# GpSimd's descriptor reserve cut to 1 KB, two more weight tiles, and the keys of two steps loaded instead of turned

## The chip, the core and the metric

The kernel runs on one core of a Trainium2 chip. The metric is the device time of one launch in microseconds (us); three runs of the kernel before gave 157.57 us as their median (156.55 to 157.78).

The core has a matrix engine (TensorE, PE in the profile, its weight loads PEld), a vector engine (VectorE, DVE), a scalar engine (ScalarE, ACT), GpSimd (POOL), and SyncE (SP), whose instruction queue starts every data transfer (DMA) of this kernel. 16 DMA engines carry the transfers; data passes through an on-chip memory (SBUF) that the kernel divides into pools of tiles, and matrix results through PSUM banks.

## The reference

A retention layer (linear attention with a decay for each head) over 4 batches, 8 heads, 768 positions and head width 64 makes `x`, and a soft mixture of 8 experts with 4 slots each is applied to its 3072 tokens of width 512.

```python
for t in range(S):
    state = gamma[None, :, None, None] * state + np.einsum('bhd,bhe->bhde', k[:, :, t], v[:, :, t])
    y[:, :, t] = scale * np.einsum('bhd,bhde->bhe', q[:, :, t], state)
...
logits = x @ phi                      # 3072 x 32
d = softmax of logits over the tokens
slot_input = d.T @ x                  # 32 x 512
for e in range(E):
    h = np.maximum(slot_input[e] @ w1[e], 0.0)      # w1: 8 x 512 x 1024
    slot_out[e] = h @ w2[e]                         # w2: 8 x 1024 x 512
c = softmax of logits over the slots
return (c @ slot_out)
```

Everything is float32. The two expert weights are 16.8 MB each, q, k and v 6.3 MB each, and so is the output.

## The kernel before

**The first part, the retention.** It runs in 24 steps (`NSTEP`), one for each batch and block of 128 positions, batches innermost, taken in pairs: pass `P` of the loop at L480 computes steps 2P and 2P+1 and prepares 2P+2 and 2P+3. A step needs q and k with the head's width on the partitions (`qT`, `kT`, side by side in the tile), v, and, for the state that is carried to the next block, k in its natural order (`kn`). All four have a place in one tile of 8 KB a partition from the pool `inp`, which has `NIN` = 6 tiles; so a step's load (`load_in`, called for steps 2P+6 and 2P+7) waits on SP until the step six before it has let go of its tile.

**Where `kn` comes from.** For a step in `TURNED`, `kn` isn't loaded: one DMA of 768 KB brings k, q and v (L210), and `turn_k` (L218) makes `kn` by four transposes on TensorE (L221) and one copy on ScalarE (L222). For the other steps one DMA of 1024 KB brings all four (L216). The last four steps (20 to 23) need no `kn`, and that place of their tiles takes the first w2 weights (L213).

**The order of a pass on each engine** is the order of the code, since the kernel is scheduled by hand on all engines: on TensorE `carry_mm` (L266), `attend_mm` (L275), `state_mm` (L303), `turn_k` (L221), `natural_mm` (L319), in every second pass the routing products (L399, L343), and `score_mm` of the next two steps (L242); on GpSimd the decays of the next steps' q (L227) and v (L232).

**The second part, the experts.** w1 is used in 16 tiles of 1024 KB by `hidden` (L637), w2 in 128-row pieces by the products at L715, in three blocks of output columns; each block's result is multiplied with the routing (L696), copied to output tiles (L703) and written by eight DMAs of 768 KB (L704).

**Where weights are loaded.** They have a pool `big` of `NBIG` = 13 tiles of 8 KB a partition. `PACE[P]` says how many tiles pass P asks for (`load_weights`, L483; w1 tiles are issued at L170, w2 tiles at L173). With that table passes 0 to 8 fill the 13 tiles, pass 9 asks for none, and pass 10 for two that go into tiles that steps have let go of, since from pass 9 on `weight_pool` is `inp`. The last w1 tile comes in halves (L187), early w2 pieces come behind the last steps into their tiles (`load_behind`, L193), two w2 tiles come as halves in the pool `ring` (L182). What is left, ten w2 tiles, is loaded at L173 in the loop over `hidden`, each into the tile of a w1 tile that was just used.

SP issues all of these in program order, so a load whose tile is still in use holds up all loads behind it.

**The reserve.** `_bacc.Bacc(...)` at L778 sets aside 16 KB of each partition for descriptors of DMAs that GpSimd starts. This kernel starts none from there.

Of the kernel before, what the change touches and what calls it, by code (L numbers as in the profile page):

```python
# [39 lines left out]
GRP = B  # L40
NGRP = NSTEP // GRP
ORDERED = "all"
NBIG = 13
NIN = 6
NRING = 9
PACE = (1, 1, 1, 2, 1, 2, 1, 2, 2, 0, 2, 0)
TURNED = (0, 1, 2, 3, 4, 6, 8, 10, 12, 14, 16)
SIW = 48
LEAN = [i for i in range(1, NSTEP) if i in TURNED or i >= NSTEP - B]
FULL = [i for i in range(1, NSTEP) if i not in LEAN]  # L50
# [32 lines left out]
def retention_soft_moe_kernel(  # L83
# [17 lines left out]
    inp = ctx.enter_context(tc.tile_pool(name="inp", bufs=NIN))  # L101
    big = ctx.enter_context(tc.tile_pool(name="big", bufs=NBIG))
    ps = ctx.enter_context(tc.tile_pool(name="ps", bufs=1, space=PSUM))
# [61 lines left out]
    def load_weights(n):  # L165
        for _ in range(n):
            which, *at = weights.pop(0)
            t = large(weight_pool[0])
            if which == "w1":
                nc.sync.dma_start(t, w1[tuple(at)])  # L170
                w1t[tuple(at)] = [t[:, j * 512:(j + 1) * 512] for j in range(4)]
            else:
                nc.sync.dma_start(t, w2[w2n[0]])  # L173
                w2n[0] += 1
                take(keys_of(*at), t)
# [42 lines left out]
    def turn_k(i, name):  # L218
        kp = bank(name)
        for g in range(NPAIR):  # L220
            nc.tensor.transpose(kp[:, g * 128:(g + 1) * 128], st[i]["kT"][:, g, :], ident)  # L221
        nc.scalar.copy(st[i]["kn"], kp.rearrange("p (h d) -> p h d", d=D))  # L222
# [83 lines left out]
    def state_add(P):  # L306
        for k in range(2):
            d = sst[(2 * P + k) % B]
            if P < B // 2:
                nc.scalar.copy(d, pr[P]["S"][:, k])  # L310
            else:
                nc.vector.tensor_tensor(d, d, pr[P]["S"][:, k], ALU.add)  # L312
# [167 lines left out]
    for P in range(NPP):  # L480
        last = P == NPP - 1
        g = P // 2
        load_weights(PACE[P])  # L483
        if P == NPP - 2:
# [45 lines left out]
        if P < NPP - B // 2:  # L530
            state_mm(P)
            state_add(P)
        if 2 * P + 2 in TURNED:
            turn_k(2 * P + 2, "A0")
# [255 lines left out]
```

## Time and profile before

| | before |
|---|---|
| median of three runs | 157.57 us |
| the profiled execution: its own time | 157.36 us |
| its span, first to last instruction | 155.7 us |
| TensorE busy | 143.1 us, 92% of the span |
| TensorE in the chain that ended last | 87% of the span |
| VectorE, GpSimd, ScalarE busy | 78.1, 58.7, 43.9 us |
| moved by DMA | 61.70 MB, 396 GB/s over the span |
| read from HBM, written to it | 55.05 MB, 6.29 MB |
| granted TensorE clock, mean | 0.985 |

A row of the timeline gives start and length of a run of like instructions; a DMA's start is that of its issue on SP. A row on DMA issues gives the median time from issue to landing; where the window holds one issue, it is that transfer's. Issue plus that time is when the transfer had landed, and landings of neighbours in the queue show how fast the queue drains.

### The profile page before, as it was taken

How to read it: one execution, taken by the hardware profiler on the slowest of the kernel's cores; microseconds unless marked ns; L12 is line 12 of the kernel's file. 1: busy time of each engine (PE TensorE's matmuls, PEld its weight loads, DVE VectorE, ACT ScalarE, POOL GpSimd, SP SyncE). 2: the span in 40 equal slices, each digit the busy share in tenths (PEclk: the TensorE clock that was granted, in tenths of full speed). 3: DMA queues.
4: the chain of work that ended last, by engine and by line, in shares of the span. 5: the costliest groups of instructions: out<-in, count | busy, mean ns of one | idle time of the engine just before them, and what ended most of it. 6: DMA issues, size and time to landing. Idle time of an engine off the chain costs nothing.

```text
span 155.7 us, 5529 instructions
## 1 busy us (share of the span) xinstructions
PE 143.1 (92%) x2424; PEld 106.9 (69%) x2424; DVE 78.1 (50%) x187; ACT 43.9 (28%) x104; POOL 58.7 (38%) x67
## 2 busy tenths in 40 slices
PE   7999999999999899999999979999999999999800
PEld 2689989997999678897989758865333465556400
DVE  0369327582948286564947584557520202563710
ACT  3214432425152403433232204341500000442510
POOL 1352987687838069912968085000200000000000
PEclk9999999999999999999999999999999999999985
DMA  5999999999999999999999999999999999999994
GB/s 165 414 428 418 427 407 429 405 431 406 421 411 420 416 417 417 415 415 422 400 416 412 416 414 356 350 278 374 404 434 419 432 411 425 415 411 422 389 422 174
DMA packets 10392, 61.70 MB, mean 396 GB/s; under 512 B 1152, under 2 KB 1152, under 8 KB 6016
## 3 DMA queue, kind: packets, MB, share of 16 engines
q1 hardware_dynamic: 10368, 61.35, 97.1%
q8 instruction: 19, 0.31, 0.8%
q14 instruction: 5, 0.04, 0.1%
HBM read 55.05 MB, written 6.29 MB: 394 GB/s over the span
## 4 chain that ended last, share of the span: by engine, by line
PE 87%; DMA 2%; DVE 2%; issue 2%; POOL 2%; DVEq 0%
PE A L242 15%; PE Y L275 14%; PE A L715 9%; PE A L319 7%; PE S L303 6%; PE Y L266 6%; PE Y L637 4%; PE A L637 4%; PE sm L343 4%; PE A L221 3%; PE S L399 3%; DMA b<-in_first_dram 2%; POOL b L227 2%; DVE b L703 2%; PE A L696 1%
## 5 line engine op out<-in xcount | busy, mean ns | idle before, releaser
L250 DVE TENSOR_TENSOR r<-A,mi 128x512 f32<-128x512 f32 (+1 forms) x50 | 30.2, 662 | 23.4 <-PE A L242 23.4
L227 POOL TENSOR_TENSOR b<-b,qtab 128x512 f32<-128x512 f32 x20 | 25.5, 1278 | 11.7 <-DMA b<-in_x_dram 4.3
L242 PE MATMUL A<-b 64*128 64x128 f32 x384 | 25.5, 280 | 0.3 <-DMA b<-in_first_dram 0.3
L242 PEld LDWEIGHTS A<-b 64*128 64x128 f32 x384 | 22.6, 187 | 3.6 <-issue 2.0
L232 POOL TENSOR_TENSOR b<-b,kt 128x512 f32<-128x512 f32 x23 | 23.8, 1052 | 2.2 <-DMA b<-in_x_dram 2.2
L275 PE MATMUL Y<-r,b 128*64 128x128 f32 x352 | 21.9, 276 | 0.7 <-POOL b L227 0.7
L275 PEld LDWEIGHTS Y<-r,b 128*64 128x64 f32 x352 | 19.0, 137 | 2.7 <-issue 1.5
L445 POOL TENSOR_TENSOR cn<-cn,cz 128x128 f32<-128x128 f32 x6 | 2.4, 401 | 34.1 <-DVE cz L444 17.7
L715 PE MATMUL A<-b,r 128*32 128x128 f32 (+1 forms) x352 | 14.4, 304 | 0.1
L715 PEld LDWEIGHTS A<-b,r 128*32 128x32 f32 x352 | 9.6, 110 | 6.2 <-issue 3.8
L326 ACT COPY r<-A 128x512 f32<-128x512 f32 x21 | 11.4, 595 | 4.3 <-PE A L319 4.3
L266 PE MATMUL Y<-b,sst 64*64 64x128 f32 x304 | 11.0, 276 | 1.0 <-issue 1.0
L319 PE MATMUL A<-mi,r 128*128 128x128 f32 x88 | 11.8, 276 | 0.0
L303 PE MATMUL S<-b 128*64 128x64 f32 x304 | 11.1, 222 | 0.8 <-issue 0.8
L303 PEld LDWEIGHTS S<-b 128*64 128x64 f32 x304 | 10.4, 138 | 1.1 <-issue 1.1
L319 PEld LDWEIGHTS A<-mi,r 128*128 128x128 f32 x88 | 9.7, 141 | 0.6 <-issue 0.4
L266 PEld LDWEIGHTS Y<-b,sst 64*64 64x64 f32 x304 | 8.4, 132 | 2.5 <-issue 1.3
L295 DVE COPY r<-Y 128x512 f32<-128x512 f32 x9 | 6.2, 692 | 6.7 <-PE Y L275 5.8
L703 ACT COPY b<-A 128x384 f32<-128x384 f32 x10 | 4.4, 483 | 17.2 <-PE A L696 16.2
L312 DVE TENSOR_TENSOR sst<-sst,S 128x256 f32<-128x256 f32 x16 | 6.0, 418 | 3.1 <-PE S L303 3.1
L696 PE MATMUL A<-cT,r 32*128 32x384 f32 x30 | 7.4, 526 | 0.0
L437 ACT ACTIVATE cn<-cn 128x128 f32<-128x128 f32 x6 | 1.9, 310 | 19.6 <-DVE cn L436 19.6
(154 smaller groups left out, 181.4 us busy)
## 6 DMA issues: line engine op xcount, KB each, us to landing
b<-in_w_dram SPq DMA_DIRECT2D x25, 1024.0 KB, 13.6
b<-in_x_dram SPq DMA_DIRECT2D x14, 768.0 KB, 10.0
b<-in_x_dram SPq DMA_DIRECT2D x9, 1024.0 KB, 11.0
out_dram<-b SPq DMA_DIRECT2D x8, 768.0 KB, 7.6
b<-in_wl_dram SPq DMA_DIRECT2D x4, 768.0 KB, 7.0
r<-in_w_dram SPq DMA_DIRECT2D x5, 512.0 KB, 9.6
b<-in_wq_dram SPq DMA_DIRECT2D x4, 256.0 KB, 11.3
b<-in_first_dram SPq DMA_DIRECT2D x1, 512.0 KB, 3.8
```

The source lines that it names most:

```text
L227: nc.gpsimd.tensor_tensor(q, q, qtab, ALU.mult)
L232: nc.gpsimd.tensor_tensor(v, v, vsc[:, i // B, a:b].unsqueeze(2).broadcast_to([128, b - a, D]), ALU.mult)
L242: nc.tensor.matmul(s["sc"][r][:, g, :], s["kT"][half(r), g, :], s["qT"][half(r), g, :], start=True, stop=True, skip_group_check=True)
L250: nc.vector.tensor_tensor(s["A"][:, r, g:g + n], s["sc"][r][:, g:g + n], mask.unsqueeze(1).broadcast_to([128, n, C]), ALU.mult)
L266: nc.tensor.matmul(p["y"][k][b][half(half_of(r, g)), gl, :], sst[(2 * P + k) % B][half(r), g, :], s["qT"][half(r), g, :], start=(gl == 0 a ...
L275: nc.tensor.matmul(pr[P]["y"][k][g // 2][half(half_of(r, g)), g % 2, :], s["v"][:, 2 * g + r, :], s["A"][:, r, g, :], start=(P < B // 2 an ...
L303: nc.tensor.matmul(S_[half(r), k, g, :], s["kn"][:, 2 * g + r, :], s["v"][:, 2 * g + r, :], start=True, stop=True, skip_group_check=True)
L319: nc.tensor.transpose(X[k][:, g * 128:(g + 1) * 128], pr[P]["yT"][:, k, g, :], ident)
L326: (nc.scalar.copy if engines[k] == "scalar" else nc.vector.tensor_copy)(xn, pr[P]["X"][k])
L637: nc.tensor.matmul(hp[hf][32 * j:32 * j + 32, :], si0[:, a:a + NSLOT], w1t[hf, g, k][j], start=(g == 0 and k == 0), stop=(g == 1 and k == ...
L696: nc.tensor.matmul(cp, s4[32 * j:32 * j + 32, m * 128:(m + 1) * 128], cT[32 * j:32 * j + 32, 3 * h:3 * h + 3, :], start=True, stop=True, s ...
L715: nc.tensor.matmul(op[32 * j:32 * j + 32, :w], hT[fc // 4][:, fc % 4, 4 * g + j, :], w2t[4 * g + j, cb, fc], start=(n == 0), stop=(n == le ...
```

## The change

Four edits, in three places. The reserve for GpSimd's descriptors is 1 KB a partition, not 16. The pool `big` has 15 tiles, not 13. `PACE` asks for two tiles in pass 9, which asked for none. Steps 14 and 16 leave `TURNED`, so `load_in` brings their `kn` by DMA and `turn_k` isn't called for them.

```diff
-NBIG = 13
+NBIG = 15
 NIN = 6
 NRING = 9
-PACE = (1, 1, 1, 2, 1, 2, 1, 2, 2, 0, 2, 0)
-TURNED = (0, 1, 2, 3, 4, 6, 8, 10, 12, 14, 16)
+PACE = (1, 1, 1, 2, 1, 2, 1, 2, 2, 2, 2, 0)
+TURNED = (0, 1, 2, 3, 4, 6, 8, 10, 12)
...
-    nc = _bacc.Bacc("TRN2", target_bir_lowering=False, num_devices=1)
+    nc = _bacc.Bacc("TRN2", target_bir_lowering=False, num_devices=1, dynamic_dma_scratch_size=1024)
```

On SP, the difference from the loads of step 13 to the end of the program (`b` is a tile of `inp` or `big`, `r` one of `ring`; `in_x` is a step's input, `in_w` weights):

```order
 L216 DMA b<-in_x_dram 128x2048
 L170 DMA b<-in_w_dram 128x2048
-L210 DMA b<-in_x_dram 128x1536
-L216 DMA b<-in_x_dram 128x2048
+L216 DMA b<-in_x_dram 128x2048 x2
 L170 DMA b<-in_w_dram 128x2048 x2
-L210 DMA b<-in_x_dram 128x1536
-L216 DMA b<-in_x_dram 128x2048
+L216 DMA b<-in_x_dram 128x2048 x2
 L170 DMA b<-in_w_dram 128x2048
 L216 DMA b<-in_x_dram 128x2048 x2
```

The loads of steps 14 and 16 grow from 1536 to 2048 columns, at the place in the queue where they stood. Further on, from the last step's load to the end:

```order
 L213 DMA b<-in_wq_dram 128x512
 L170 DMA b<-in_w_dram 128x2048 x2
+L173 DMA b<-in_w_dram 128x2048 x2
 L187 DMA r<-in_w_dram 128x1024
 L193 DMA b<-in_wl_dram 128x1536 x2
@@ -40,5 +39,5 @@
 L193 DMA b<-in_wl_dram 128x1536 x2
 L182 DMA r<-in_w_dram 128x1024 x4
-L173 DMA b<-in_w_dram 128x2048 x10
+L173 DMA b<-in_w_dram 128x2048 x8
 L704 DMA out_dram<-b 128x1536 x8
```

Two tiles of 1024 KB move from the ten behind the first expert products to the place ahead of the last w1 tile: pass 9 now loads the two w1 tiles that pass 10 loaded, and pass 10 two w2 tiles. On TensorE, pass 6 before, from the state's products to the scores of step 14:

```order
L303 MATMUL S<-b 64x64 x16
L221 MATMUL A_995<-mi,b 128x128 x4
L319 MATMUL A_1001<-mi,r 128x128 x4
L319 MATMUL A_1006<-mi,r 128x128 x4
L379 MATMUL sm<-mi,pT 128x128
L242 MATMUL A_1018<-b 128x128
```

and now:

```order
L303 MATMUL S<-b 64x64 x16
L319 MATMUL A_995<-mi,r 128x128 x4
L319 MATMUL A_1000<-mi,r 128x128 x4
L379 MATMUL sm<-mi,pT 128x128
L242 MATMUL A_1012<-b 128x128
```

The four transposes at L221 are gone here, as in pass 7, and with each four the copy at L222 on ScalarE. GpSimd's order is the same.

## Rows read from the trace of the kernel before

**Rows 1.** DMA queue of the data transfers, whole span: packets, MB, share of engines.

```profile
q1 hardware_dynamic: 10368, 61.35, 97.1%
```

**Rows 2.** Stretches: length; PE, PEld, DVE, ACT, POOL busy (count); clock, DMA share, GB/s.

```profile
94.00:99.00 5.00, 5.00 (x89) 4.42 (x89) 2.77 (x6) 1.93 (x4) 1.45 (x3) 1.00 0.96 374
99.00:104.00 5.00, 5.00 (x97) 3.71 (x89) 2.64 (x8) 1.97 (x6) 0.00 (x0) 1.00 0.91 267
...
109.00:146.00 37.00, 36.31 (x574) 18.01 (x562) 11.17 (x33) 7.70 (x17) 0.80 (x2) 1.00 1.02 419
```

**Rows 3.** Timeline of SP, 94 to 109 us: start, length, engine, line, transfer, count.

```profile
94.61 0.83 SPq L193 DMA_DIRECT2D b<-in_wl_dram  x2
99.43 0.33 SPq L187 DMA_DIRECT2D sst<-in_w_dram  x1
100.48 1.78 SPq L193 DMA_DIRECT2D b<-in_wl_dram  x2
...
108.68 0.33 SPq L173 DMA_DIRECT2D b<-in_w_dram  x1
```

**Rows 4.** DMA issues at 94.61, 99.43, 100.48, 108.68: size, us to landing.

```profile
b<-in_wl_dram SPq DMA_DIRECT2D x1, 768.0 KB, 5.8
...
sst<-in_w_dram SPq DMA_DIRECT2D x1, 512.0 KB, 4.9
...
b<-in_wl_dram SPq DMA_DIRECT2D x1, 768.0 KB, 6.9
...
b<-in_w_dram SPq DMA_DIRECT2D x1, 1024.0 KB, 8.4
```

**Rows 5.** Issues at 3.33, 3.83; 61.32, 61.77; 113.83, 114.69; q8 in 0:71, 0:133, 94:109.

```profile
b<-in_x_dram SPq DMA_DIRECT2D x1, 768.0 KB, 10.0
...
b<-in_x_dram SPq DMA_DIRECT2D x1, 1024.0 KB, 13.2
...
b<-in_x_dram SPq DMA_DIRECT2D x1, 1024.0 KB, 6.8
...
b<-in_x_dram SPq DMA_DIRECT2D x1, 1024.0 KB, 10.4
...
b<-in_w_dram SPq DMA_DIRECT2D x1, 1024.0 KB, 18.2
...
b<-in_w_dram SPq DMA_DIRECT2D x1, 1024.0 KB, 20.5
...
q8 instruction: 9, 0.15, 0.9%
...
q8 instruction: 17, 0.28, 0.9%
...
q8 instruction: 2, 0.03, 1.1%
```

**Rows 6.** The chain that ended last, passes 7, 9 and 10: start, us, what.

```profile
69.06 0.59 PE A L221 x4
69.64 0.87 PE A L319 x8
...
85.76 1.02 PE A L319 x8
...
91.65 1.04 issue
```

**Rows 7.** Sixth output's issue; its landing; the very first load's landing.

```profile
146.59 0.33 SPq L704 DMA_DIRECT2D out_dram<-b  x1
...
out_dram<-b SPq DMA_DIRECT2D x1, 768.0 KB, 4.6
...
b<-in_first_dram SPq DMA_DIRECT2D x1, 512.0 KB, 3.8
```

**Rows 8.** Step 23: GpSimd's decay of q; the chain's row of its scores.

```profile
91.79 1.27 POOL L227 TENSOR_TENSOR b<-b,qtab 128x512 f32<-128x512 f32 x1 [0.74 <-DMA b<-in_x_dram]
...
97.25 1.09 PE A L242 x16
```

## The prediction

> **What bounds the kernel now.** I read the DMA queue first. The data queue moves 61.35 MB [rows 1]. In a stretch in which it is always fed, 109 to 146 us, it moves 419 GB/s [rows 2]. 61.35 MB at that rate are 146.4 us of a span of 155.7, so the queue has 9 us to spare in the whole execution, the start and the last landing among them. TensorE is busy for 92% of the span by the page's first part, and the chain that ended last runs on it for 87%. So two clocks run side by side, the queue and TensorE, and a saving on one of them is worth only what the other lets through.
>
> Then I asked where the queue loses time. At 419 GB/s a load of 1024 KB takes 2.50 us, 768 KB 1.88, 512 KB 1.25, 256 KB 0.63. Two kinds of loss stand out.
>
> First, a hole between 94 and 104 us: 374 GB/s, then 267 [rows 2]. SP issues at 94.61 the next load, at 99.43 one, at 100.48 two [rows 3], each as soon as the last steps let go of a tile. With their times to landing [rows 4] they have landed at 100.4, 104.3 and 107.4, and the first weight tile issued at 108.68 at 117.1. From 100.4 to 117.1 the queue delivered 768 + 512 + 1536 + 2048 + 1024 = 5888 KB, which takes 14.4 us at the full rate and took 16.7: **2.3 us lost**. Most of it is in two places: 3.9 us where 1280 KB should take 3.1, and 3.1 us where 768 KB should take 1.9. The load issued at 99.43 landed 4.9 us later, and the very first one, with nothing ahead of it, took 3.8 [rows 7], so there was about 1 us of work ahead of it: the queue was nearly empty. Part of the 16 engines ran dry already at 94 to 99, where the rate sinks.
>
> Second, jumps in the landings. Issues at 3.33 and 3.83 landed at 13.3 and 17.0, 3.7 us apart where 2.5 are due: 1.2 lost. Those at 61.32 and 61.77 landed at 68.1 and 72.2: 1.5 lost. Those at 113.83 and 114.69 landed at 132.0 and 135.2: 0.7 lost [rows 5]. The q8 instruction packets reach nine by 71 us and seventeen by 133 [rows 5], eight apart, just as the second and the third jump come. I read this as instruction packets of 16 KB that go round eight engines; a transfer has landed when its slowest engine has, so only the packets that hit the engine already slowest move the landings. The third jump is smaller because the hole let the slow engines catch up.
>
> **The reserve and the pool.** GpSimd starts no DMA in this kernel, so the smaller reserve takes nothing from it; it pays for two tiles of 8 KB. I cost it at nothing: no row shows a transfer that would use it.
>
> **Two weight tiles early.** In pass 9 SP issues 2 x 1024 KB right behind step 23's load, which is before 94.61, and neither waits for a step's tile, since the pool has two new ones. That puts 5.0 us of work ahead of the loads of [rows 3]. At 99.43 there would be about 6 us ahead, not 1, so the hole closes: 2.3 us back. The same tiles go missing from the ten at L173, where the queue has 16 us and more ahead of it (18.2 and 20.5 us to landing [rows 5]), so nothing starves there. The cost is the third jump: with the hole gone the slowest engine stays slowest, and the seventeenth packet costs it the mean of the first two, 1.35, not 0.7: 0.65. The bounds of that term are 0 and 0.8.
>
> **Keys of steps 14 and 16.** The DMA queue carries 2 x 256 KB more: 2 x 0.63 = 1.25 us, in a queue that is full there, so all of it shows behind. TensorE loses in passes 6 and 7 the four transposes, 0.59 us each pass, but the products behind them, which wait for the copies of the attention, take 1.02 in a pass without `turn_k` (pass 9) and 0.87 in one with it (pass 7) [rows 6]: 0.59 + 0.87 - 1.02 = 0.44 a pass, 0.88 in all. Two copies on ScalarE go as well; it is busy for 43.9 us of 155.7 and I give them nothing. The later loads of steps are up to 1.25 us late: GpSimd's decay of step 23 waits 0.74 us for its load already and ends at 93.06, while its scores start at 97.25 [rows 8]. Against a TensorE that is 0.88 earlier there are still 4.2 - 1.25 - 0.88 = 2.1 us of cover; were it gone, each 1 us would cost TensorE 1 us. Nothing is late on that account.
>
> **The end.** The sixth output is issued at 146.59 and lands at 151.2 [rows 7]. A load with nothing ahead took 3.8 us for 512 KB, so 768 KB would take 4.4 and land at 151.0: the two clocks meet there within 0.2 us. With the change the queue is earlier by 2.3 - 0.65 - 1.25 = 0.4 (landing at 150.8), TensorE's side by 0.88 (150.1). The queue sets the end, and the last two outputs follow at 1.88 each as before.
>
> The sum: **-0.4 us** on the profiled execution's 157.36, 157.0 us. The median of the runs is 0.21 above that execution, so **157.2 us**. If TensorE gained nothing, its 151.0 would bind and the gain would be 0.2; so this forecast hardly hangs on the transposes.
>
> The Trainium skill, HBM Reference, Specifications (TRN2), gives a core about 358 GB/s as its share of a pair and about 425 when it streams alone. This trace's 419 sides with the second. At 358 the two keys would cost 1.46 us, which as an estimate from that page would make the sum -0.2.
>
> **Rivals.** *A, the third jump stays 0.7.* Then the queue gains 2.3 - 1.25 = 1.05 and TensorE's side allows 1.1: 156.5 us. For it: 0.7 is the only third jump that was measured. Against: it came behind the hole, which goes.
>
> *B, slower: the loss in the hole is not for want of work.* Two q8 packets fall into 94 to 109 us [rows 5], and a jump there may be theirs as much as the empty queue's. What decides is how much of the 2.3 comes back: below 1.25 + 0.65 = 1.9 the kernel is slower. With none back it is +1.25 if the third jump stays, 158.8, and +1.9 if it grows, 159.5. Against it: the rate sinks at 94 to 99 while the landing at 100.4 is still on time, which is how engines look that have nothing to do. The Trainium skill, DMA: Bandwidth & Descriptors, Queues, rings and completion order, says that each DMA engine takes turns between its queues packet by packet; by that rule instruction packets delay data as in B whether the queue is full or not, and the time would be B's. The jumps [rows 5] agree with the rule, and no row shows how much of the hole it makes.
>
> *C, TensorE waits longer for no visible reason.* Its chain has a wait of 1.04 us marked issue [rows 6]. The instructions taken out shift what follows, and full queues may lengthen such waits. One more of 1.04 eats the 0.88 and lands the sixth output at 151.2, no gain; two more cost 0.9: 157.6 to 158.5.
>
> *D, more than 1% faster.* No third jump at all (the packet meets another engine) and that wait of 1.04 gone: the queue gains 2.3 + 0.7 - 1.25 = 1.75, TensorE's side 0.88 + 1.04 + 0.2 = 2.1: 155.8 us. Nothing speaks for the coincidence but that both are matters of position.
>
> **Chances.** The forecast 0.48 (alone 156.8 to 157.6, which takes in the bounds of its jump and of TensorE's part), A 0.18, B 0.12, C 0.12, D 0.10. The range leaves out D and the far part of B: 156.1 to 158.6. About 1%, 1.6 us, is what a measurement of this kernel can tell from no change. Faster by more: D and the edge of A, 0.12. Slower by more: most of B, 0.10. Within: 0.78.
>
> **What the profile would show.** The hole: the rate between 94 and 109 us should be 415 GB/s or more, and the loads issued there should take 9 us or more to land; if it stays under 390, B holds. The queue: the sixth output should land near 150.8 instead of 151.2. The jump: near 133 us two neighbours should land 3.7 to 4.0 us apart; 3.2 speaks for A. TensorE: no L221 behind step 12, the products of passes 6 and 7 at 1.02, the last block of the experts 0.9 earlier; if it is later, C. The end: the outputs should land 1.8 to 1.9 apart through the sixth; if the sixth comes late, TensorE bound it, not the queue.

## The result and the profile after

The changed kernel takes 157.62 us (median of 22 runs, 157.16 to 158.78); the kernel before, timed beside it, 156.55 us (22 runs, 156.07 to 158.24). The ratio is 1.0064, 95% interval 1.0042 to 1.0086: **1.0 us slower**, where the prediction had 0.4 us faster. Within 1% it is, but on the other side, and the three runs shown ahead of the prediction (157.57) were from the upper part of what the kernel before does: its median over all later runs is 156.5. That 157.62 lies only 0.4 us from the forecast 157.2 is luck: the forecast started 1.0 us too high and moved the wrong way.

The profiled execution of the changed kernel took 157.95 us (span 156.2); that of the kernel before 157.36. The queue and the stretches of [rows 1, 2], now (packets, MB, share; then length, busy time of PE, PEld, DVE, ACT, POOL with counts, clock, DMA share, GB/s):

```profile
q1 hardware_dynamic: 10368, 61.87, 96.6%
...
94.00:99.00 5.00, 5.00 (x88) 4.30 (x82) 3.02 (x6) 2.26 (x7) 3.30 (x4) 1.00 1.02 418
...
99.00:104.00 5.00, 5.00 (x89) 3.83 (x83) 2.63 (x8) 1.97 (x6) 0.00 (x0) 1.00 1.01 411
```

0.52 MB more are moved, and the hole is closed: 418 and 411 GB/s where 374 and 267 stood. SP's timeline there (start, length, line, transfer, count), and behind it the times to landing of the issues at 94.38, 99.18, 100.23, 109.22, 115.55 and 116.81, as in [rows 3 to 5]:

```profile
83.44 1.15 SPq L170 DMA_DIRECT2D b<-in_w_dram  x2
86.64 2.86 SPq L173 DMA_DIRECT2D b<-in_w_dram  x2
...
94.38 0.81 SPq L193 DMA_DIRECT2D b<-in_wl_dram  x2
99.18 0.33 SPq L187 DMA_DIRECT2D sst<-in_w_dram  x1
100.23 0.33 SPq L193 DMA_DIRECT2D b<-in_wl_dram  x1
```

```profile
b<-in_wl_dram SPq DMA_DIRECT2D x1, 768.0 KB, 12.9
...
sst<-in_w_dram SPq DMA_DIRECT2D x1, 512.0 KB, 11.2
...
b<-in_wl_dram SPq DMA_DIRECT2D x1, 768.0 KB, 12.1
...
b<-in_w_dram SPq DMA_DIRECT2D x1, 1024.0 KB, 12.6
...
b<-in_w_dram SPq DMA_DIRECT2D x1, 1024.0 KB, 16.2
...
b<-in_w_dram SPq DMA_DIRECT2D x1, 1024.0 KB, 19.1
```

The four early tiles go out in time, and the loads of the last steps wait 11 to 13 us in a full queue. From 94.38 + 12.9 = 107.3 to 109.22 + 12.6 = 121.8 the same 5888 KB as before take 14.5 us; 14.4 are due, so 0.1 is lost where 2.3 were. The third jump is there: 115.55 + 16.2 = 131.8, 116.81 + 19.1 = 135.9, in the unrounded trace 4.2 us apart, 1.7 lost where 0.7 were.

TensorE's side, from the chain that ended last (start, us, what), passes 6 and 7, 9 and 10, and the last expert block:

```profile
62.31 1.02 PE A L319 x8
...
69.29 1.02 PE A L319 x8
...
84.99 0.72 issue
...
92.60 0.42 issue
...
143.03 0.34 issue
```

The transposes are gone, at the price foreseen (1.02 for 0.59 + 0.87, [rows 6]); the wait of 1.04 at 91.65 is gone too, and others stand in pass 9, pass 10 and at 143 (0.72, 0.42, 0.34), so that the last block of the experts is not 0.9 us earlier but 0.5 later. The end, to be held against [rows 7]: the sixth output's issue, and the times to landing of the fifth (issued at 142.04) and of the sixth:

```profile
147.06 0.33 SPq L704 DMA_DIRECT2D out_dram<-b  x1
...
out_dram<-b SPq DMA_DIRECT2D x1, 768.0 KB, 7.9
...
out_dram<-b SPq DMA_DIRECT2D x1, 768.0 KB, 4.7
```

Fifth and sixth land at 149.9 and 151.8, 1.8 apart, the queue's own pace: the queue sets the end, 0.6 us later than before (151.2), although the closed hole, the grown jump and the cheaper passes of the prediction are all to be seen in this trace.

### The profile page after: what moved, and what is told of

Its sections match the earlier page's. It is cut to its first block, busy times and chain, and to the rows that moved or that the text cites. A ratio compares the mean times of both kernels' runs of the same rounds, so it can differ in the third digit from the quotient of the medians.

```text
span 156.2 us, 5502 instructions
## 1 busy us (share of the span) xinstructions
PE 143.8 (92%) x2416; PEld 107.0 (68%) x2416; DVE 77.7 (50%) x187; ACT 43.0 (28%) x102; POOL 58.6 (38%) x67
## 4 chain that ended last, share of the span: by engine, by line
PE 89%; DVE 2%; issue 2%; POOL 2%; DVEq 0%
PE A L242 16%; PE Y L275 14%; PE A L715 9%; PE A L319 7%; PE S L303 6%; PE Y L266 6%; PE Y L637 4%; PE A L637 4%; PE sm L343 4%; PE sm L453 3%; PE S L399 3%; PE A L221 2%; POOL b L227 2%; DVE b L703 2%; PE A L696 1%
## 5 line engine op out<-in xcount | busy, mean ns | idle before, releaser
L242 PE MATMUL A<-b 64*128 64x128 f32 x384 | 26.4, 286 | 0.0
L242 PEld LDWEIGHTS A<-b 64*128 64x128 f32 x384 | 23.4, 193 | 3.3 <-issue 2.2
L275 PE MATMUL Y<-r,b 128*64 128x128 f32 x352 | 22.2, 276 | 1.1 <-POOL b L227 0.6
L275 PEld LDWEIGHTS Y<-r,b 128*64 128x64 f32 x352 | 19.0, 137 | 3.4 <-issue 2.2
L366 ACT ACTIVATE pT<-sm,nm 128x128 f32<-128x128 f32 x4 | 1.5, 367 | 20.9 <-PE Y L275 10.6
## 6 DMA issues: line engine op xcount, KB each, us to landing
r<-in_w_dram SPq DMA_DIRECT2D x5, 512.0 KB, 12.6
b<-in_wq_dram SPq DMA_DIRECT2D x4, 256.0 KB, 12.6
```

Source lines behind the costliest of these rows:

```text
L242: nc.tensor.matmul(s["sc"][r][:, g, :], s["kT"][half(r), g, :], s["qT"][half(r), g, :], start=True, stop=True, skip_group_check=True)
L275: nc.tensor.matmul(pr[P]["y"][k][g // 2][half(half_of(r, g)), g % 2, :], s["v"][:, 2 * g + r, :], s["A"][:, r, g, :], start=(P < B // 2 an ...
```

## The experiments

Two theories stood against each other. *Queue*: the DMA queue sets the end, and its bytes and stalls decide. *TensorE*: its chain sets the end, and the change only moved its waits. A ratio is always to the kernel before on the same chip.

### The two halves of the change, and the reserve

**Keys alone.**

```diff
-TURNED = (0, 1, 2, 3, 4, 6, 8, 10, 12, 14, 16)
+TURNED = (0, 1, 2, 3, 4, 6, 8, 10, 12)
```

> The kernel before with one edit: steps 14 and 16 leave TURNED, so their keys come by DMA; pool, pace and reserve stay. Queue theory (the DMA queue sets the end, TensorE is close behind): the hole between 94 and 109 us stays, because nothing new is issued ahead of it, and 512 KB more go through a queue that is full at that place; +1.25 us less what the later arrival fills of the hole, so +0.6 to +1.25 us, ratio 1.004 to 1.008. TensorE theory (TensorE sets the end): the transposes' 0.88 us come off, ratio 0.994, unless the instructions that are gone shift a wait marked issue into the last expert block as in the changed kernel, which gives 1.000 to 1.003 and such a wait near 143 us.

Measured: 158.11 us, ratio 1.0091 (1.0059 to 1.0123). TensorE had the transposes taken off and the kernel became 1.4 us slower. So the bytes cost at least what the queue theory said, whose range ended at 1.008. In the profile the hole is open (362 GB/s between 94 and 109 us) and the sixth output takes 5.5 us to land, so it waits for the queue; the time does not show that any of the bytes vanish into the hole.

**Weight tiles alone.**

```diff
-NBIG = 13
+NBIG = 15
-PACE = (1, 1, 1, 2, 1, 2, 1, 2, 2, 0, 2, 0)
+PACE = (1, 1, 1, 2, 1, 2, 1, 2, 2, 2, 2, 0)
-    nc = _bacc.Bacc("TRN2", target_bir_lowering=False, num_devices=1)
+    nc = _bacc.Bacc("TRN2", target_bir_lowering=False, num_devices=1, dynamic_dma_scratch_size=1024)
```

> The kernel before with the reserve of 1 KB, 15 weight tiles and two tiles in pass 9; TURNED stays. Queue theory: the hole closes (415 GB/s between 94 and 109 us), 2.2 us come back, the third jump grows from 0.7 to 1.7, the queue is about 1.2 us earlier, and TensorE's side, which does not move, lets 0.2 to 0.3 of it through: ratio 0.992 to 0.999, the sixth output issued at the same time as before and landing 4.4 us later. TensorE theory: ratio 1.000, no more. If the ratio is above 1.002, closing the hole itself costs something that neither theory has.

Measured: 156.14 us, ratio 0.9971 (0.9950 to 0.9993). Its stretch from 94 to 109 us, its sixth output and that output's time to landing:

```profile
94.00:109.00 15.00, 15.00 (x219) 10.42 (x218) 9.63 (x28) 5.83 (x18) 1.93 (x4) 1.00 1.01 415
...
145.89 0.33 SPq L704 DMA_DIRECT2D out_dram<-b  x1
...
out_dram<-b SPq DMA_DIRECT2D x1, 768.0 KB, 4.2
```

The hole is closed, and it brings 0.45 us (0.1 to 0.8 by the interval), a quarter of the 1.65 net that the prediction had for it. The two halves add up: 0.9 to 1.0% for the keys, -0.3% for the tiles, 0.6% together. Also worth seeing: its 12 runs lie between 155.86 and 156.49, 34 of the 35 of the kernel before between 155.82 and 157.69.

**One tile.** `NBIG = 14` and a 1 in place of the new 2 in `PACE`, reserve 1 KB.

> The kernel before with the reserve of 1 KB, 14 weight tiles and one tile in pass 9: half the early weights, no keys by DMA. If the hole is for want of work, half of it closes: between 94 and 109 us 370 to 400 GB/s (336 before, 414 in the changed kernel), ratio 0.997 to 0.999. If what comes back is capped by TensorE, one tile is as good as two: 0.997.

Measured: 155.98 us, ratio 0.9978 (0.9951 to 1.0005), 413 GB/s between 94 and 109 us. One tile closes the hole as well as two, so half of the early load was more than was needed. TensorE is not the cap: the sixth output lands 4.1 us after its issue in this profile and 4.2 with two tiles, and outputs below land after 3.3, so in both it waits for the queue.

**Reserve alone.**

```diff
-    nc = _bacc.Bacc("TRN2", target_bir_lowering=False, num_devices=1)
+    nc = _bacc.Bacc("TRN2", target_bir_lowering=False, num_devices=1, dynamic_dma_scratch_size=1024)
```

> The kernel before with the reserve of 1 KB alone. Nothing uses the reserve, so both theories give a ratio of 1.000 (0.998 to 1.002), and the trace is a second execution of the schedule before: the hole at 94 to 109 us and the three jumps in the landings show how much of them repeats. A rival, that the move of the pools in SBUF costs or brings something, needs a ratio outside that.

Measured: 156.44 us, ratio 0.9988 (0.9967 to 1.0008). By itself the reserve does nothing that shows.

### Bytes or transposes

**The changed kernel with its transposes put back.** The keys of 14 and 16 are loaded and turned.

```diff
-        if 2 * P + 2 in TURNED:
+        if 2 * P + 2 in TURNED + (14, 16):
```

> The changed kernel, with the transposes of steps 14 and 16 put back: their keys come by DMA and are then turned on TensorE all the same. Against the kernel with the weight tiles alone (0.9971) it differs by 512 KB of loads and nothing else. Queue theory: it is as slow as the changed kernel, ratio 1.005 to 1.008, because the transposes are hidden behind the queue. TensorE theory: 0.9 us slower than the changed kernel, 1.012; or the instruction positions are back and it is near 1.000.

Measured: 157.45 us, ratio 1.0073 (1.0046 to 1.0099): the changed kernel's time, with all the work on TensorE that it had saved. Sixth output, issue and time to landing:

```profile
147.75 0.33 SPq L704 DMA_DIRECT2D out_dram<-b  x1
...
out_dram<-b SPq DMA_DIRECT2D x1, 768.0 KB, 3.3
```

It is issued 0.7 us later than in the changed kernel's profile and lands 0.7 earlier. So an output can land 3.3 us after its issue, not 4.4 at the least as the prediction had it.

**Keys of step 14 alone.** The kernel with the two tiles, and only step 14 out of `TURNED`.

> The kernel with the two early weight tiles, and the keys of step 14 by DMA, those of step 16 turned: half of the changed kernel's bytes. If bytes set the end, it lies half way between the kernel with the weight tiles alone (0.9971) and the changed one (1.0064): 1.000 to 1.003. If one of the two steps does the harm by where it stands, or the instructions taken out, it is near one of the two.

Measured: 156.74 us, ratio 1.0022 (1.0006 to 1.0037): half way between 0.9971 and 1.0064. That is 0.4 to 0.5% for each 256 KB.

**Fewer transposes, no byte more.** The kernel with the two tiles, and in `turn_k`:

```diff
+        if i in (14, 16):
+            nc.tensor.transpose(kp[:, 0:128], st[i]["kT"][:, 0, :], ident)
+            kn = st[i]["tile"][:, 1536:2048].rearrange("p (g t) -> p g t", t=C)
+            nc.scalar.copy(kn, kp[:, 0:128].unsqueeze(1).broadcast_to([128, NPAIR, C]))
+            return
```

> The kernel with the weight tiles alone, and in steps 14 and 16 one transpose in place of four, its result copied to all four places (three quarters of the keys of these two steps are left out, and no byte more is loaded). TensorE has 0.6 to 0.9 us less to do, the queue is as it was. If TensorE holds back what the closed hole gave the queue, the ratio falls below 0.9971, to about 0.993. If the queue holds it, 0.997 again. If the changed kernel is slow for want of these instructions, 1.003 or more.

Measured: 156.59 us, ratio 0.9998 (0.9975 to 1.0021), against 0.9971 with all the transposes. Less work on TensorE did not help; whether it did a little harm the intervals don't tell. Its profile is of its longest execution (157.30 us). There TensorE is later than in the kernel with the tiles alone, through other waits: its chain has 0.37 and 0.44 us marked issue at 78.85 and 86.12, and TensorE waits 0.8 us for VectorE. The sixth output's issue (145.89 with the tiles alone), and the times to landing of the fifth (issued at 143.43) and the sixth:

```profile
147.73 0.33 SPq L709 DMA_DIRECT2D out_dram<-b  x1
...
out_dram<-b SPq DMA_DIRECT2D x1, 768.0 KB, 5.0
...
out_dram<-b SPq DMA_DIRECT2D x1, 768.0 KB, 3.3
```

They land at 148.4 and 151.0, 2.6 us apart and not 1.8. So in this execution TensorE sets the end: with the hole closed and no byte more, the queue is ahead of it by 0.7 us.

**The opposite edit: step 18 turned too**, 256 KB less, in the kernel before:

```diff
-TURNED = (0, 1, 2, 3, 4, 6, 8, 10, 12, 14, 16)
+TURNED = (0, 1, 2, 3, 4, 6, 8, 10, 12, 14, 16, 18)
```

> The kernel before with step 18 turned too: 256 KB less, nothing else. Queue theory: 0.6 us less at the end, less what the hole takes, because work ahead of the late loads is 0.6 us shorter while TensorE lets go of their tiles 0.44 us later: ratio 0.996 to 1.000, and 1 us or more lost between the landing near 100 us and the first weight tile behind the expert products. TensorE theory: 1.003.

Measured: ratio 0.9971 (0.9948 to 0.9995), but this kernel's executions fall into two groups, eight of 155.50 to 156.71 us and four of 158.89 to 159.51, and the ratio is that of the first. In the first group fewer bytes are a little faster. The profile is of the second group, with waits marked issue of 1.01 at 85.73 and 1.33 at 93.35 us, the loads of the last steps issued at 96.26 and 101.43, and a hole of 282 GB/s between 94 and 109. No execution of the first group was profiled, so it is not shown that these waits part the groups.

**Step 18 turned, with the two tiles.**

> The opposite of the changed kernel's last edit: the two early weight tiles stay, and step 18 is turned on TensorE as well, so that 256 KB less are loaded (TURNED ends in 14, 16, 18). Queue theory, with what the bytes cost so far (0.9 to 1.0% for 512 KB): the queue is 0.6 to 0.75 us earlier, ratio 0.992 to 0.995, as far as TensorE, 0.44 us later, lets it through. If TensorE now sets the end: ratio 0.999 to 1.001, the sixth output issued 0.4 us later than in the kernel with the weight tiles alone and landing about 4.2 us after its issue.

Measured: six runs, one of 155.46 us and five of 157.85 to 159.45; no ratio. Nothing is settled on the average. In the profiled execution (159.45) the sixth output is issued at 149.78, just as the fifth lands at 149.8. There TensorE sets the end.

### What the hole is worth: the schedule before, again

The early tiles closed the hole and gave back little. So I took further profiles of the kernel before.

> The kernel before, unchanged, for another profile. The one that the prediction was read from took 157.36 us, 0.8 us above the median of the later runs. If its losses were those of a slow execution, this one shows less than 2.3 us lost between the landing at 100.4 us and the first weight tile behind the expert products, or other jumps in the landings; if they repeat, 2.0 to 2.5 us.

Measured: 156.22 us. Stretch, SP's issues, and the times to landing of those at 97.91 and 98.96 (that at 93.09 took 7.4):

```profile
94.00:109.00 15.00, 15.00 (x216) 10.02 (x216) 9.87 (x30) 4.99 (x15) 1.86 (x4) 1.00 1.01 387
...
93.09 0.83 SPq L193 DMA_DIRECT2D b<-in_wl_dram  x2
97.91 0.33 SPq L187 DMA_DIRECT2D sst<-in_w_dram  x1
98.96 1.20 SPq L193 DMA_DIRECT2D b<-in_wl_dram  x2
...
sst<-in_w_dram SPq DMA_DIRECT2D x1, 512.0 KB, 5.7
...
b<-in_wl_dram SPq DMA_DIRECT2D x1, 768.0 KB, 6.5
```

Landings at 100.5, 103.6 and 105.5: 3.1 us for 1280 KB and 1.9 for 768, the full pace. **Nothing is lost at these two places**, where the prediction's execution lost most of its 2.3 us. By the prediction's own measure, the 5888 KB up to the first weight tile behind the expert products, it is 0.35 us, since that tile landed at 115.2, 14.75 us behind the landing at 100.4:

```profile
107.15 0.33 SPq L173 DMA_DIRECT2D b<-in_w_dram  x1
...
b<-in_w_dram SPq DMA_DIRECT2D x1, 1024.0 KB, 8.0
```

The rate still sinks to 387 GB/s, because engines that are ahead run dry; the one that lands last does not. The trace shows it in the sixteen reports that it has of each transfer, of which the last is the landing: first and last report lie 3.3 us apart at 102.3 and 1.8 at 107.4, while the landings keep their pace. TensorE was 1.5 us earlier than in the profile that the prediction was read from. From 84 to 91.6 us the chains of the two executions run within 0.1 us of each other; then one has the wait of 1.04 and the other none. The products at L275 behind it, in the prediction's execution and in this one:

```profile
93.13 1.90 PE Y L275 x32
...
91.60 1.90 PE Y L275 x32
```

A second such profile, and two with the same loads and a few instructions more or fewer at the start:

> The kernel before, unchanged, a fourth profile of its schedule. Where the loads behind the last steps were issued at 94.6 and 99.4 us the slowest engine lost 2.2 us, at 94.4 and 99.2 about 1.0 and at 93.1 and 97.9 nothing. If the loss is set by how late TensorE lets go of the tiles, this execution follows that order: nothing lost where more than 4.4 us of work are ahead of the load at 98 to 99 us, 0.5 us or more where it is under 3.5.

```diff
     warm(WARM)
+    warm(2, w=64)
```

> The kernel before with two more warm-up products of 64 columns at the start, where TensorE waits for the first load: eight TensorE instructions more, nothing else. Position theory: waits marked issue of 1 us near 87 and 95 us appear, as in the kernels with step 18 turned, TensorE lets go of the last steps' tiles 2 us later, the hole between 94 and 109 us deepens to under 340 GB/s, and executions near 158 to 159 us appear. If position does not matter: ratio 1.000.

```diff
-    warm(WARM)
+    warm(2, w=512)
```

> The kernel before with two warm-up products of 512 columns in place of four of 256: eight TensorE instructions fewer, the same columns. Half of the shift of the changed kernel, without its loads. Position theory, weak form: the waits move but do not grow, ratio 0.998 to 1.003. If the changed kernel's loss of 0.6% were the shift of its instructions and not its bytes, this one would show part of it: 1.003 or more.

The second repeat took 156.54 us. Ratios: 0.9994 (0.9961 to 1.0028) with eight TensorE instructions more, 0.9993 (0.9956 to 1.0030) with eight fewer. Shifts of eight do not change the time, and the waits of 1 us that I expected of the first did not come. What the profiles give is a row of executions of one schedule of loads, in order of their time. The last column is what the landings lose against the full pace behind the one near 100 us: over the 5888 KB, and in a jump behind them.

| profiled execution | time, us | 512 KB load issued at | GB/s, 94 to 109 us | lost, us |
|---|---|---|---|---|
| before, again (first) | 156.22 | 97.91 | 387 | 0.35 + 1.25 |
| before, again (second) | 156.54 | 98.03 | 380 | 0.5 + 1.25 |
| eight instructions more | 156.78 | 98.50 | 373 | 2.3 + 0 |
| reserve alone | 157.15 | 99.24 | 359 | 2.3 + 0 |
| before, the prediction's | 157.36 | 99.43 | 337 | 2.25 + 0.65 |
| eight instructions fewer | 157.94 | 99.91 | 320 | 2.7 + 0.4 |

The last of them, stretch, issues, and landings of those at 99.91 and 100.96:

```profile
94.00:109.00 15.00, 15.00 (x232) 11.29 (x232) 8.80 (x24) 5.81 (x18) 1.73 (x3) 1.00 0.93 320
...
95.09 0.82 SPq L193 DMA_DIRECT2D b<-in_wl_dram  x2
99.91 0.33 SPq L187 DMA_DIRECT2D sst<-in_w_dram  x1
...
sst<-in_w_dram SPq DMA_DIRECT2D x1, 512.0 KB, 5.4
...
b<-in_wl_dram SPq DMA_DIRECT2D x1, 768.0 KB, 6.7
```

The later TensorE lets go of the last steps' tiles, the later the load, the deeper the hole and the longer the execution: 2.0 us later, 1.7 us longer. The order is the same in the first three columns, and the loss grows with them from 1.6 to 3.1 us. In all six the sixth output lands 4.4 to 5.1 us after its issue, so the queue sets the end. With "eight more" and "reserve alone" the jump comes early: 1.7 and 1.3 us of their 2.3 are one jump at 113 to 114 us, inside the stretch, and none follows near 133. With the two early tiles the same sum is 0.2 + 1.5, with one 0.1 + 1.6, in the changed kernel 0.15 + 1.7. By these sums, closing the hole gives back 1.2 us of the prediction's execution and nothing of the plain repeats. The load issued at 95.09 took 5.6 us and landed at 100.7; the 768 + 512 KB behind it take 3.1 us at the full pace and would have landed at 103.8, and they landed at 99.91 + 5.4 = 105.3: 1.5 us lost here.

### TensorE's position, twice more

**Sixteen instructions put back at the start of the changed kernel.**

```diff
     warm(WARM)
+    warm(4, w=64)
```

> The changed kernel with four more warm-up products of 64 columns (16 TensorE instructions) at the start, where TensorE waits for the first load anyway. They put about as many instructions back into TensorE's stream as the transposes took out, ahead of everything. If the wait marked issue near 143 us (0.34 us, 0.7 us lost in the last expert block) comes from where the instruction blocks end, it goes away and the waits stand where they stood before: TensorE's end 0.5 to 0.7 us earlier. Then, if TensorE set the end of the changed kernel, its ratio to before falls from 1.006 to 1.002; if the queue set it, it falls to 1.004 at most and the sixth output is issued earlier but lands as late.

Measured: 157.57 us, ratio 1.0062 (1.0040 to 1.0085), the changed kernel's. Sixth output:

```profile
146.42 0.33 SPq L705 DMA_DIRECT2D out_dram<-b  x1
...
out_dram<-b SPq DMA_DIRECT2D x1, 768.0 KB, 4.7
```

The wait at 143 us is gone from this profile, the output is issued 0.64 us earlier, and it waits for the queue as long as before. It also lands 0.66 earlier, since the third jump is 0.9 us here and not 1.7. 4.7 us from issue to landing, with 3.3 possible, say that the queue sets the end in both profiles.

**Step 18 turned, with the two tiles, and eight instructions fewer at the start.**

> The kernel with the two early weight tiles and step 18 turned, and two warm-up products of 512 columns at the start in place of four of 256: eight TensorE instructions fewer ahead of everything, as many as the transposes of step 18 add behind. If the waits marked issue (1.01 us near 87 us, 1.33 near 95 in that kernel, 0.2 and none in the one without step 18) come with the place of the instructions in TensorE's stream, they go, and the saved bytes show: ratio 0.992 to 0.995, sixth output issued near 146.3. If the waits belong to the transposes of step 18 themselves, the executions stay near 158 us.

Measured: one run of 155.31 us, eleven of 157.32 to 158.30. The ratio, over the six shortest, is 1.0013 (0.9959 to 1.0067); it mixes the one with five of the eleven, so nothing is read from it. Of its chain, and its sixth output:

```profile
85.83 0.90 issue
...
93.42 1.14 issue
...
148.47 0.33 SPq L704 DMA_DIRECT2D out_dram<-b  x1
...
out_dram<-b SPq DMA_DIRECT2D x1, 768.0 KB, 3.3
```

The two waits are still there: eight instructions fewer at the start did not take them away. The fifth output landed at 148.7, 3.1 us ahead of the sixth, so TensorE sets the end in this execution too.

## Why the prediction was wrong

**The hole's worth: the step that failed.** "2.3 us back" was read rightly from the trace and taken for a property of the kernel. It was one of that execution, in which TensorE had been held up by a wait marked issue (1.04 us at 91.65) and let go of the last steps' tiles 1.5 us later than in the first repeat. By the same measure the two plain repeats lost 0.35 and 0.5 us. Measured, the closed hole is worth 0.45 us on the average of the runs, jump included, where the prediction had 2.3 - 0.65. I even wrote that this execution lay 0.21 us below the median of the runs shown; both were from the upper part of a spread of 155.8 to 158.2 us.

**A rate is not a landing.** The sentence "the rate sinks at 94 to 99 while the landing at 100.4 is still on time, which is how engines look that have nothing to do" was right, and I should have carried it further: in the first repeat 387 GB/s cost 0.35 us at the most. What counts is when the slowest engine runs dry.

**The third jump** was taken as a cost of closing the hole (0.65). It did grow, from 0.7 to 1.7 us in the changed kernel. But where the hole had cost the slowest engine little, as in the plain repeats, the third jump was full already (1.25 us); it belongs to the same execution as the 2.3, and the two must be taken or left together. As a sum of 2.3 - 0.65 they came out nearly four times the average.

**The keys' bytes** were 1.25 us by the rate and cost 0.9 to 1.0%, 1.4 to 1.6 us: keys alone 1.0091 against 1, with the tiles 1.0064 and 1.0073 against 0.9971. Right in kind, somewhat small in size; the intervals (0.3% each) do not exclude 1.25, and where another 0.2 would come from stays open.

**The sum** with measured terms is -0.45 for the tiles and +1.42 for the keys alone, +1.0 us, which is the result. The point from which rival B decides was named as 1.9 us of the 2.3, which is 1.25 net of the jump; 0.45 net came back. B ends on the right side, at 158.8 on the wrong starting time, but not for its reason: in the first repeat, too, two q8 packets fall between 94 and 109 us, and the landings at 103.6 and 105.5 are on time. So the packets alone do not make the loss, and it is not there in every execution. Whether one of them had a share of it in the prediction's execution is not shown.

**TensorE's savings** of 0.44 us a pass are in the trace, and are worth nothing that shows: the kernel with the transposes put back (1.0073) is not clearly slower. The prediction had them as hardly mattering, but thought TensorE's side only 0.2 us from binding. It took 4.4 us from issue to landing as the least for an output; 3.3 occurs in four profiles, so in the prediction's execution, with 4.6, TensorE had over 1 us of slack. It is no more than that: where TensorE is 1 to 2 us later, as in the profile with fewer transposes, it does set the end.

**Rival C**, longer waits on TensorE: they did move (0.34 us at 143 in the profile), and in the execution without that one the time was the changed kernel's all the same. (C's own sum for two more waits of 1.04 should read 1.0, not 0.9.) **Rival A** is refuted by the jump of 1.7; with the hole closed and step 18 loaded, seven profiles have 0.9 to 1.7. **The reserve** costs nothing, as said. With the hole closed the queue moves 411 to 418 GB/s. The Trainium skill, HBM Reference, Specifications (TRN2), gives about 425 for a core that streams alone; this trace agrees.

**What makes TensorE wait** can be read from the traces by counting its instructions from the first one profiled, weight loads and the sequencer's own included. The 17 profiles have 46 waits marked issue of more than 0.2 us ahead of a TensorE product. Each stands at instruction 193 + 256 k or the next one (k is 6, 7, 10, 11, 12 or 18), and each ends 1.2 to 1.6 us after the q8 packet number k has been moved. So a packet of 16 KB brings TensorE 256 instructions over the same DMA engines as the data, and TensorE waits where its packet is late. In the prediction's execution the twelfth packet moved at 90.2 us, 5.2 us after TensorE had begun the block before, and the wait ended at 92.69; in the first repeat it moved after 2.5 us, and there is no wait. The place in the stream does decide where a wait can be. The four shifts of 8 or 16 instructions were too small to test that, as they move the edge of a block by eight products at the most.

**What stays open** is why the same packet comes late in one execution and not in the next, and why in the three kernels with step 18 turned many executions, or most, are 2 to 4 us longer than the shortest.

## What to carry to other kernels

Before a stall in one profile is priced, ask whether the next execution has it: where runs of a kernel spread by 1 to 2%, take a second profile, and price what both show. Where the last outputs wait for the queue, as in most profiles here, bytes are time and work on an engine is not, up to the slack of about 1 us that their times to landing show. The edit worth having here is the early weight tiles alone (0.9971); one tile may do (0.9978, but its interval reaches 1.0005), and the keys should stay on TensorE. A sagging mean rate (387 GB/s) cost 0.35 us at the most here, so look for late landings instead. And a wait that nothing in the profile ends can be a wait for instructions: count them.

## What the hardware showed

The queue's landings are so regular (2.5 us for 1024 KB) that a jump of 0.9 to 1.7 us stands out; such jumps recur near the first and the ninth instruction packet in most profiles here, and near the seventeenth in many. Between the jumps first and last report of a transfer keep their distance: in the first repeat 0.6 us, 1.8 behind the first jump, 3.2 behind the second. TensorE's instructions come in 19 packets of 16 KB an execution, through the data's engines, and it waits up to 1.33 us for a late one. An output of 768 KB landed 3.3 us after its issue when the queue was nearly empty, while the first load of 512 KB took 3.3 to 3.9. And six executions of one schedule of loads differed by 1.7 us, in step with when one load could be issued.
